# Attention, then a gated MLP, on one core: smaller transposed pieces at the start, a transposing DMA replaced by matmuls, the last product in two halves

## The chip, the cores and the metric
The kernel runs on one core of a Trainium2 chip. The metric is the device time of one execution in microseconds; below it is compared as the median of several runs. Engines: TensorE (PE in the rows, its weight loads PEld), VectorE (DVE), ScalarE (ACT), GpSimd (POOL, nearly unused here) and SyncE (SP), whose queue issues nearly all DMAs.

## The reference
q, k and v are 4 batches of 12 heads, 448 positions, 64 wide, in f32. All attention weights are sigmoids, so there is no sum over a row:

```python
scores = q @ k.T / sqrt(64) - log(448)
attn = 1 / (1 + exp(-scores))
x = (attn @ v)              # to 1792 tokens x 768
xn = x / sqrt(mean(x*x) + 1e-6) * rms_g
g = xn @ w_gate             # 768 x 1536
out = (silu(g) * (xn @ w_val)) @ w_out   # 1536 x 768
```

## The kernel before
Matmul operands are split into a high and a low f16 part, and a product of two such pairs takes three matmuls (`PARTS`: high by high, high by low, low by high).

**Attention** (0 to 139 us). The 48 heads are 12 units of four heads; a unit has 7 slots (c), and a slot's scores are 12 matmuls on 64-row quarters of the array into two PSUM banks, read by one sigmoid of 896 columns on ScalarE (L278). Slots are taken in pairs over all 84: scores of two slots, then attention times v (`av`, L289) for the two slots of the pair before. With 7 slots to a unit, (4,6) and (5,0) are one pair. After each slot's scores the list `FILL[c]` runs what is due in that slot, most of it for a unit two ahead: splitting q and k of that unit into high and low (`qk_hi`, `qk_lo`, L223 and L227, VectorE), issuing the DMA that transposes them (`transpose`, L232, SP), and issuing loads. For unit 0, `transpose_here` transposes raw f32 q and k by matmuls with an identity (L244), evicts the high part on ScalarE (L248) and makes the low part on VectorE (L249). For the units in `ON_PE` (q and k of 1, q of 2) `on_pe` transposes the split halves by f16 matmuls, 4 blocks and then 3 (`PIECES`), and copies the high part on ScalarE (L260) and the low part on VectorE (L258); each call takes 0.5 from `credit[0]`. Small PSUM results (transposes, `av` sums, norms) share four banks (tag "m"); a unit's `av` holds two of them.

After each slot and each `av`, `run_later` adds 0.8 to `credit[0]` (at most 2.5) and 0.18 to the credit of ScalarE's parts (at most 0.6), and takes parts from three queues (sums of squares, norms, weight splits) as long as the credit is above zero. The norm of one batch: sums of squares on TensorE (`squares`, L342), small steps on VectorE, a matmul that spreads the reciprocal root (`rows`, L380, copied by ScalarE at L381), then scaling and splitting (L384 on). Weight splits put the high part on ScalarE (L485).

**The MLP** (to the end). Products by a Winograd scheme for w_gate and w_val (L511) from 142 us, then 8 plain output products (L600), then five pairs of token tiles with w_out by the same scheme (`product_o`, L697). `pair_rest` runs a pair's products into banks "ob", "od" and "oc"; VectorE adds each to `u` (L736), and `store` issues the halves of the tile as two DMAs. The last product of the last pair, `product(pc, 6, 2, True)`, adds to bank "oc", which product (3, 3) began; its store goes out by SP and by ScalarE's queue.

Of the kernel before, what the change touches and what calls it, by code (L numbers as in the profile page):

```python
# [12 lines left out]
AF = mybir.ActivationFunctionType  # L13
ALU = mybir.AluOpType


SQ = 2.0**6
# [7 lines left out]
def attention_then_swiglu(  # L25
# [21 lines left out]
    nc = tc.nc  # L47
    B, H, S, D = q.shape
    DFF, DM = w_out.shape
    P = 128  # L50
    NPAIR = H // 2
    NSLOT = 2 * S // P
# [5 lines left out]
    HALF = DM // 2  # L58
# [8 lines left out]
    ps_m = ctx.enter_context(tc.tile_pool(name="ps_m", bufs=4, space=bass.MemoryType.PSUM))  # L67

    WARM, BETWEEN = 6, 2
    SPLIT_AT = (12, 30)  # L70
    ON_PE = ((1, 0), (1, 1), (2, 0))
    PIECES = (0, 4), (4, 3)
    MID = 3
    SLOT = 0.8
    ACT_SLOT = 0.18

# [6 lines left out]
    ident = const.tile([P, P], F32, name="ident")  # L83
# [90 lines left out]
    def bank(name):  # L174
        return ps_m.tile([P, 512], F32, tag="m", name=name)
# [4 lines left out]
    stt = nc.vector.scalar_tensor_tensor  # L180
# [3 lines left out]
    at, pav = {}, {}  # L184
# [44 lines left out]
    def transpose(u, t):  # L229
        if (u, t) in ON_PE:  # L230
            return
        nc.sync.dma_start_transpose(  # L232
            out=t_b[u % 3][:, t].rearrange("p l c r -> p (l c) r"),
            in_=nat(u)[:, t].rearrange("p l c d -> p (l c d)"),
        )

    def transpose_here(u, t):
        src, dst = raw(u, t), t_b[u % 3][:, t]
        ps = [bank("tr") for _ in range(2)]
        for c in range(NSLOT):  # L240
            half_, at = divmod(c, MID + 1)
            for r in range(2):
                o = ps[half_][D * r : D * r + D, at * P : at * P + P]
                nc.tensor.matmul(o, src[:, r, c], ident, start=True, stop=True)  # L244
        for half_ in range(2):
            n = MID + 1 - half_
            hi, lo = (dst[:, l, half_ * (MID + 1) : half_ * (MID + 1) + n].rearrange("p c r -> p (c r)") for l in range(2))
            nc.scalar.activation(hi, ps[half_][:, : n * P], AF.Copy, scale=SQ)  # L248
            stt(lo, ps[half_][:, : n * P], SQ, hi, ALU.mult, ALU.subtract)  # L249

    def on_pe(u, t, begin, n):
        for l in range(2):
# [253 lines left out]
    def product(ps, fc, n, a, b, more=False):  # L506

        w = win[fc % 2]
        for c in range(NK):
            for m, (l, r) in enumerate(PARTS):  # L510
                nc.tensor.matmul(  # L511
                    ps,
                    w[:, l, b, c],
                    xc[n, a][:, r, c],
                    start=(not more and c == 0 and m == 0),
                    stop=(c == NK - 1 and m == 2),
                    skip_group_check=more,
                )
# [136 lines left out]
    def sums_h(p, t):  # L655

        f11, f12, f21, f22 = hf_b
        s22, s11, s21, s12 = hs_b[p % 2]

        def add(o, f0, f1, op, cost):  # L660
            return lambda: tt(o, f0, f1, op), cost

        def hi(s, f):
            return lambda: nc.scalar.activation(s[:, 0], f, AF.Copy), 0.0

        parts = []
        for f, tile_, i in ((f21, t + 1, 0), (f22, t + 1, 1), (f11, t, 0), (f12, t, 1)):
            for m, k, parts_ in h_whole(tile_, i):
                parts.append(add(f[:, m : m + k], *parts_, ALU.add, 0.1 + 0.14 * k))
        parts += [add(f22, f21, f22, ALU.add, 0.97), hi(s22, f22)]  # L670
        parts += [add(f21, f11, f21, ALU.subtract, 0.97), hi(s21, f21)]
        parts += [add(f11, f22, f11, ALU.subtract, 0.97), hi(s11, f11)]
        parts += [add(f12, f12, f11, ALU.subtract, 0.97), hi(s12, f12)]
        los = [add(s[:, 1], f, s[:, 0], ALU.subtract, 0.91) for s, f in ((s11, f11), (s21, f21), (s22, f22), (s12, f12))]
        return [(x, cost, ("f", p)) for x, cost in parts] + [(x, cost, (p, n)) for n, (x, cost) in enumerate(los)]
# [10 lines left out]

    unit_o = 1.0 / (SH * SO)

    def product_o(p, t, ps, x, y, more=False):
        def a(m, l):  # L690
            return hs_b[p % 2][x - 3][:, l, m] if x > 2 else h_part(2 * m + (x > 0), l, t + (x == 2))

        w, i, e = (
            (wo, 0, 0), (wo, 1, 0), (wo, 1, 1), (wt, 0, 0), (wt, 0, 1), (wt, 1, 1), (wt, 1, 0))[y]
        for m in range(NFC // 2):
            for n, (l, r) in enumerate(PARTS):
                nc.tensor.matmul(  # L697
                    ps[:, :HALF],
                    a(m, l),
                    w[2 * m + i][:, r, e * HALF : e * HALF + HALF],  # L700
                    start=(not more and m == 0 and n == 0),
                    stop=(m == NFC // 2 - 1 and n == 2),
                    skip_group_check=more,
                )
# [20 lines left out]
    def pair_rest(p, t):  # L725

        def product(ps, x, y, more=False):
            if x in (4, 5, 3, 6):
                run_line((p, (4, 5, 3, 6).index(x)))
            product_o(p, t, ps, x, y, more)  # L730
            clock["pe"] += HALF_PROD
            run_line()
            clock["dve"] = max(clock["dve"], clock["pe"]) + 0.56

        def add(o, ps, u):
            stt(two(o), two(ps[:, :HALF]), unit_o, u, ALU.mult, ALU.add)  # L736

        u = u_o[p]
        c22, c21, c12 = (next_o() for _ in range(3))
        pb = bank("ob")  # L740
        product(pb, 4, 5)
        stt(u, two(pb[:, :HALF]), unit_o, u, ALU.mult, ALU.add)
        pd, pc = banks("od")[:, 0], banks("oc")[:, 0]
        product(pd, 5, 4)
        add(c22, pd, u)
        product(pc, 3, 3)
        add(c22, pc, two(c22))
        store(c22, t + 1, 1)
        product(pd, 2, 6, True)
        add(c21, pd, u)  # L750
        store(c21, t + 1, 0)
        product(pc, 6, 2, True)
        add(c12, pc, u)
        store(c12, t, 1, True)

    n_out = [0]

# [6 lines left out]
        nc.scalar.activation(o, ps[:, :HALF], AF.Copy, scale=unit_o)  # L764
        store(o, t, e)

    def store(o, t, e, last=False):
        cols = slice(e * HALF, e * HALF + HALF)
        rows = out.rearrange("(b p c) d -> b c p d", b=B, c=NSLOT)
        for j in range(2):  # L770
            b, c = divmod(2 * t + j, NSLOT)
            queue = nc.scalar if last and j else nc.sync
            queue.dma_start(rows[b ^ 1, c, :, cols], o[64 * j : 64 * j + 64])


    adds, norms, splits = [], [], []
# [24 lines left out]
    def ahead_by(n, part, *t, cost=0.0):  # L801
        def run(u):
            if u + n < NU:
                part(u + n, *t)
                credit[0] -= cost

        return run

    K, Q = 1, 0
# [5 lines left out]
    def only(n, part, *which, cost=0.0):  # L815
        def run(u):
            if u == n:
                part(*which)
                credit[0] -= cost

        return run

    def from_1(n, part, *t, cost=0.0):
        run = ahead_by(n, part, *t, cost=cost)
        return lambda u: u and run(u)

    def first(*parts):
        return [only(0, x, *a, cost=cost) for x, *a, cost in parts]

    def second(*parts):  # L830
        return [only(1, x, *a, cost=cost) for x, *a, cost in parts]
# [4 lines left out]
        [from_1(2, qk_hi, Q, cost=0.53)],  # L836
        first((on_pe, 1, Q, *PIECES[0], 0.0)) + [next_v, from_1(2, qk_lo, Q, cost=1.0)],
        first((on_pe, 1, Q, *PIECES[1], 0.0), (qk_hi, 2, K, 0.53)) + [from_1(2, transpose, K)],
        first((on_pe, 1, K, *PIECES[0], 0.0), (qk_lo, 2, K, 1.0)) + second((on_pe, 2, Q, *PIECES[0], 0.0)),
        first((transpose, 2, K, 0.0)) + second((on_pe, 2, Q, *PIECES[1], 0.0)) + [from_1(2, transpose, Q), ahead_by(4, load_qk, K), from_1(4, load_qk, Q)],  # L840
    )

    make_identity(nc, ident)
# [6 lines left out]
    with tc.manual_schedule():  # L850
# [19 lines left out]
        for t in (K, Q):  # L870
            for _ in range(3):
                run_load()
            load_qk(3, t)

        transpose_here(0, Q)
        warm(BETWEEN)
        transpose_here(0, K)

        todo = [(u, c) for u in range(NU) for c in range(NSLOT)]
        split = {}  # L880
        for n in range(0, len(todo) + 2, 2):
# [12 lines left out]
            if loads and loads[0][0] < 2:  # L894
                run_load()
            if n in SPLIT_AT:
                fc = SPLIT_AT.index(n)
                split[fc] = split_w(fc)
# [60 lines left out]
        first = [(t, e) for t in range(4) for e in range(2)]  # L959
# [8 lines left out]
        for c in range(NFC):  # L968
# [10 lines left out]
                    load_o(c + 10)  # L979
            else:  # L980
                run_lo()
        pairs_o = (4, 6, 8, 10, 12)
        clock.update(pe=-1.2, dve=-11.0)
        waiting = []
        for m in range(NFC // 2):
# [2 lines left out]
                sums.extend(pair)  # L988
            line.extend((x, cost, "o") for x, cost in sums)
            waiting = los  # L990
        h0 = sums_h(0, pairs_o[0])
        line.extend(h0[:2] + [(x, cost, "o") for x, cost in waiting] + h0[2:])
        for p, t in list(enumerate(pairs_o))[1:]:
            line.extend(sums_h(p, t))
        run_line()
        for (t, e), ps in zip(first, pss):
# [1 line left out]
        clock["pe"] = 0.0  # L998

        raw = None  # L1000
        for p, t in enumerate(pairs_o):
            ps = raw_first(p, t)
            if raw:
                raw_second(*raw)
            raw = p, t, ps
        raw_second(*raw)
        for p, t in enumerate(pairs_o):
            pair_rest(p, t)


# [28 lines left out]
```

## Time and profile before

| | us |
|---|---|
| median of 3 runs | 582.74 (581.82 to 583.57) |
| the profiled execution | 582.68 |
| its span, first to last record | 580.90 |
| TensorE busy | 569.7 (98%) |
| VectorE busy | 487.0 (84%) |
| ScalarE busy | 257.7 (44%) |

The span is what the rows count from (0 is its start); 1.78 us of the profiled execution lie around it. Busy shares are averages over stages with different limits: ScalarE is near full in parts of attention and nearly idle later. "L278" is line 278 of the kernel. A name such as `sc<-xc` says what an instruction writes and reads; an arrow behind the idle time names what ended it.

### The profile page before, as it was taken

What the parts mean: (1) busy time and instruction counts of PE and PEld (TensorE: products, weight loads), DVE (VectorE), ACT (ScalarE), POOL (GpSimd) and SP (SyncE); (2) the same over time, 40 slices, a digit from 0 to 9 for tenths busy, and PEclk for the clock granted to TensorE, in tenths of its full rate; (3) what the DMA queues carried; (4) which work ended last, traced back from release to release, by engine and by line L of the source; (5) the groups of instructions that cost most, each with busy time, mean ns of one, the idle gap of its engine ahead of it and who ended that gap; (6) DMA issues with size and microseconds to landing.
All of it is one profiled execution on the core that took longest, in us unless ns stands there. A gap on an engine that the chain in (4) does not pass through costs nothing.

```text
span 580.9 us, 10382 instructions
## 1 busy us (share of the span) xinstructions
PE 569.7 (98%) x4266; PEld 311.2 (54%) x4266; DVE 487.0 (84%) x746; ACT 257.7 (44%) x376; POOL 0.7 (0%) x6
## 2 busy tenths in 40 slices
PE   8999989999999999999999999999999999999996
PEld 5455545554555555555555555555556666665664
DVE  4597898988999978888788887887789999888861
ACT  5788899976643243232332423314222354411220
POOL 0000000000000000000000000000000000000000
PEclk9999999999999999999999999999999999999999
DMA  7999999980003304134041230422173023111111
GB/s 250 229 266 233 230 288 228 161 195 1 1 1 107 93 20 109 29 80 109 1 110 48 61 109 2 108 68 88 64 299 136 1 48 88 42 42 41 42 42 41
DMA packets 70881, 59.72 MB, mean 103 GB/s; under 512 B 38063, under 2 KB 69298, under 8 KB 70834
## 3 DMA queue, kind: packets, MB, share of 16 engines
q1 hardware_dynamic: 70434, 58.58, 40.7%
q8 instruction: 33, 0.54, 0.4%
q10 hardware_dynamic: 400, 0.49, 0.2%
q14 instruction: 14, 0.11, 0.1%
HBM read 44.83 MB, written 5.51 MB: 87 GB/s over the span
## 4 chain that ended last, share of the span: by engine, by line
PE 89%; ACT 5%; DVE 2%; DMA 2%; issue 2%; SPq 0%; ACTq 0%; DVEq 0%
PE cc L511 14%; PE cd L511 14%; PE ca L511 14%; PE o L600 8%; PE av L289 7%; PE cb L511 7%; PE sc L274 5%; PE oc L697 5%; PE od L697 5%; PE oa L697 5%; ACT room L278 3%; PE ob L697 3%; DMA room<-in_k_dram 1%; DMA xc<-in_k_dram 1%; ACT room L309 1%
## 5 line engine op out<-in xcount | busy, mean ns | idle before, releaser
L511 PEld LDWEIGHTS <-wr 128*128 128x128 f16 x1512 | 147.8, 98 | 138.4 <-issue 0.7
L511 PE MATMUL ca<-xc,wr 128*128 128x448 f16 x432 | 89.6, 352 | 0.0
L278 ACT ACTIVATE room<-sc,bias_s 128x896 f32<-128x896 f32 x84 | 83.3, 1031 | 13.6 <-PE sc L274 13.2
L289 PE MATMUL av<-room 64*64 64x448 f32 x672 | 74.4, 538 | 0.0
L511 PE MATMUL cc<-xc,wr 128*128 128x448 f16 x324 | 67.2, 352 | 0.0
L511 PE MATMUL cd<-xc,wr 128*128 128x448 f16 x324 | 67.2, 352 | 0.0
L274 PE MATMUL sc<-xc 64*64 64x448 f16 x1008 | 60.8, 351 | 3.8 <-ACT room L278 2.0
L274 PEld LDWEIGHTS <-xc 64*64 64x64 f16 x1008 | 33.3, 106 | 34.3 <-issue 24.3
L539 ACT ACTIVATE room<-ca 128x448 f32<-128x448 f32 x24 | 13.0, 542 | 84.8 <-PE ca L511 84.8
L511 PE MATMUL cb<-xc,wr 128*128 128x448 f16 x216 | 44.8, 352 | 0.0
L488 DVE SCALAR_TENSOR_TENSOR wr<-wr 128x768 f16<-128x768 f32 (+1 forms) x48 | 39.1, 852 | 2.2 <-ACT wr L485 2.2
L289 PEld LDWEIGHTS av<-room 64*64 64x64 f32 x672 | 28.1, 133 | 21.6 <-issue 16.0
L600 PE MATMUL o<-xc,room 128*128 128x384 f16 x240 | 39.2, 326 | 0.0
L566 ACT ACTIVATE room<-room 128x448 f32<-128x448 f32 x24 | 13.8, 576 | 52.9 <-DVE room L565 52.9
L485 ACT ACTIVATE wr<-wr 128x768 f16<-128x768 f32 (+1 forms) x48 | 34.8, 763 | 4.9 <-DVE wr L482 4.9
L697 PEld LDWEIGHTS <-wr 128*128 128x128 f16 x246 | 24.1, 98 | 15.9
L600 PEld LDWEIGHTS <-room 128*128 128x128 f16 x240 | 23.5, 98 | 15.6
L534 DVE TENSOR_TENSOR room<-room,cb 128x448 f32<-128x448 f32 x24 | 14.9, 620 | 16.8 <-PE cb L511 16.7
L435 DVE SCALAR_TENSOR_TENSOR wr<-wr 128x768 uint32<-128x768 uint32 x28 | 26.8, 957 | 0.8
L434 DVE SCALAR_TENSOR_TENSOR wr<-wr 128x768 uint32<-128x768 uint32 x28 | 26.8, 958 | 0.6
L697 PEld LDWEIGHTS <-room 128*128 128x128 f16 x204 | 20.0, 98 | 13.2
L527 ACT ACTIVATE room<-ca 128x448 f32<-128x448 f32 x24 | 13.1, 544 | 30.2 <-PE ca L511 24.6
(161 smaller groups left out, 751.9 us busy)
## 6 DMA issues: line engine op xcount, KB each, us to landing
room<-in_v_dram SPq DMA_DIRECT2D x24, 224.0 KB, 4.5
wr<-in_moe_w_gate_dram SPq DMA_DIRECT2D x12, 384.0 KB, 3.7
wr<-in_moe_w_gate_dram SPq DMA_DIRECT2D x24, 192.0 KB, 4.2
wr<-in_moe_w_val_dram SPq DMA_DIRECT2D x12, 384.0 KB, 4.3
wr<-in_moe_w_val_dram SPq DMA_DIRECT2D x24, 192.0 KB, 4.5
wr<-in_moe_w_out_dram SPq DMA_DIRECT2D x6, 768.0 KB, 5.0
xc<-in_k_dram SPq DMA_DIRECT2D x20, 224.0 KB, 3.7
xc<-in_q_dram SPq DMA_DIRECT2D x20, 224.0 KB, 4.3
```

Source lines behind the costliest of these rows:

```text
L274: nc.tensor.matmul(o, T[rows, 1, l, c, cols], T[rows, 0, m, :, cols], start=(n == 0), stop=(n == 2))
L278: nc.scalar.activation(a, ps[:, :, :S], AF.Sigmoid, bias=bias_s, scale=1.0 / (math.sqrt(D) * SQ * SQ))
L289: nc.tensor.matmul(ps[D * (j ^ r) : D * (j ^ r) + D, :S], v_b[u % 2][rows, r, c], a[rows, r], start=(c == 0), stop=(c == NSLOT - 1),)
L434: lambda: stt(b, r[:, :, 0], 29, b, ALU.logical_shift_right, ALU.bitwise_or),
L435: lambda: stt(b, r[:, :, 1], 0xC0000000, b, ALU.bitwise_and, ALU.bitwise_or),
L485: nc.scalar.activation(t[:, 0, s], wf[:, s], AF.Copy, scale=SW)
L488: stt(t[:, 1, s], wf[:, s], SW, t[:, 0, s], ALU.mult, ALU.subtract)
L511: nc.tensor.matmul(ps, w[:, l, b, c], xc[n, a][:, r, c], start=(not more and c == 0 and m == 0), stop=(c == NK - 1 and m == 2), skip_group ...
L534: tt(u_b, u_b, pb[:, :S], ALU.add)
L566: nc.scalar.activation(y[:, 1], y[:, 1], AF.Silu, scale=UNIT)
L600: nc.tensor.matmul(ps[:, :HALF], h[c, t // NTOK][:, l, t % NTOK * P : t % NTOK * P + P], wo[c][:, r, e * HALF : e * HALF + HALF], start=(c ...
L697: nc.tensor.matmul(ps[:, :HALF], a(m, l), w[2 * m + i][:, r, e * HALF : e * HALF + HALF], start=(not more and m == 0 and n == 0), stop=(m ...
```

## The change
Three edits. (1) `transpose_here` takes a piece (a first block and a count) and one bank for each; q of unit 0 is taken in its pieces of 4 and 3 blocks, k in 2, 3 and 2. (2) (5, 0), q of unit 5, joins `ON_PE`: its DMA transpose is not issued, and `on_pe` runs for it in unit 4, in slots 5 and 6. (3) The last product of the last pair is made as two products of 192 columns, each followed by its add and its store.

```diff
-    ON_PE = ((1, 0), (1, 1), (2, 0))
+    ON_PE = ((1, 0), (1, 1), (2, 0), (5, 0))
...
-    def transpose_here(u, t):
+    def transpose_here(u, t, begin, n):
         src, dst = raw(u, t), t_b[u % 3][:, t]
-        ps = [bank("tr") for _ in range(2)]
-        for c in range(NSLOT):
-            half_, at = divmod(c, MID + 1)
+        ps = bank("tr")
+        for c in range(n):
             for r in range(2):
-                o = ps[half_][D * r : D * r + D, at * P : at * P + P]
-                nc.tensor.matmul(o, src[:, r, c], ident, start=True, stop=True)
-        for half_ in range(2):
-            n = MID + 1 - half_
-            hi, lo = (dst[:, l, half_ * (MID + 1) : half_ * (MID + 1) + n].rearrange("p c r -> p (c r)") for l in range(2))
-            nc.scalar.activation(hi, ps[half_][:, : n * P], AF.Copy, scale=SQ)
-            stt(lo, ps[half_][:, : n * P], SQ, hi, ALU.mult, ALU.subtract)
+                o = ps[D * r : D * r + D, c * P : c * P + P]
+                nc.tensor.matmul(o, src[:, r, begin + c], ident, start=True, stop=True)
+        hi, lo = (dst[:, l, begin : begin + n].rearrange("p c r -> p (c r)") for l in range(2))
+        nc.scalar.activation(hi, ps[:, : n * P], AF.Copy, scale=SQ)
+        stt(lo, ps[:, : n * P], SQ, hi, ALU.mult, ALU.subtract)
...
-        product(pc, 6, 2, True)
-        add(c12, pc, u)
-        store(c12, t, 1, True)
+        if p + 1 < len(PAIRS_O):
+            product(pc, 6, 2, True)
+            add(c12, pc, u)
+            store(c12, t, 1, True)
+        else:
+            for n in range(2):
+                cols = slice(n * HALF // 2, (n + 1) * HALF // 2)
+                product_o(p, t, pc, 6, 2, True, cols)
+                stt(c12[:, cols], pc[:, cols], unit_o, u[:, n], ALU.mult, ALU.add)
+                store(c12, t, 1, True, cols)
...
-        first(...) + second((on_pe, 2, Q, *PIECES[0], 0.0)),
+        first(...) + second((on_pe, 2, Q, *PIECES[0], 0.0)) + [only(4, on_pe, 5, Q, *PIECES[0])],
-        first(...) + second((on_pe, 2, Q, *PIECES[1], 0.0)) + [from_1(2, transpose, Q), ...],
+        first(...) + second((on_pe, 2, Q, *PIECES[1], 0.0)) + [only(4, on_pe, 5, Q, *PIECES[1]), from_1(2, transpose, Q), ...],
...
-        transpose_here(0, Q)
+        for piece in PIECES:
+            transpose_here(0, Q, *piece)
         warm(BETWEEN)
-        transpose_here(0, K)
+        for piece in ((0, 2), (2, 3), (5, 2)):
+            transpose_here(0, K, *piece)
```

`product_o` and `store` take the columns as an argument, and the list of pairs of the last stage moves to the top as `PAIRS_O`.

## Rows read from the trace of the kernel before

**Rows 1.** The page: busy time and share by engine; chain of waits, shares by engine.
```profile
PE 569.7 (98%) x4266; PEld 311.2 (54%) x4266; DVE 487.0 (84%) x746; ACT 257.7 (44%) x376; POOL 0.7 (0%) x6
...
PE 89%; ACT 5%; DVE 2%; DMA 2%; issue 2%; SPq 0%; ACTq 0%; DVEq 0%
```

**Rows 2.** Chain of waits, 0 to 145 us: start us, us, engine and line.
```profile
7.28 1.10 PE tr L244 x15
...
9.78 0.41 PE sc L274 x4
...
10.21 1.91 ACT room L278 x2
```

**Rows 3.** Waits, 44 to 48 us: who for whom, total us, times, longest.
```profile
PEld av L289 <- DMA room<-in_v_dram: 1.2, 2, 0.7
```

**Rows 4.** Line 232, 46.5 to 47.5 us: the transpose of unit 4's q.
```profile
DMA to landing us min/median/max: 5.7/5.7/5.7
```

**Rows 5.** Timeline of TensorE, 40 to 92 us: start, us, instructions, idle before and releaser.
```profile
52.64 1.42 PE L274 MATMUL sc<-xc 64*64 64x448 f16 x24
...
63.09 0.76 PE L274 MATMUL sc<-xc 64*64 64x448 f16 x12
64.89 0.76 PE L274 MATMUL sc<-xc 64*64 64x448 f16 x12 [1.04 <-DMA xc<-room]
...
82.17 0.76 PE L274 MATMUL sc<-xc 64*64 64x448 f16 x12 [0.48 <-ACT room L278]
...
85.22 1.66 PE L274 MATMUL sc<-xc 64*64 64x448 f16 x24 [0.78 <-ACT room L278]
```

**Rows 6.** Timeline of SP, 40 to 130 us: issues only, not the transfers.
```profile
58.25 2.54 SPq L232 DMA_TRANSPOSE xc<-room  x1
61.25 1.27 SPq L191 DMA_DIRECT2D xc<-in_k_dram  x2
```

**Rows 7.** Timelines of VectorE and of TensorE, 92 to 145 us.
```profile
130.02 3.03 DVE L384 TENSOR_TENSOR room<-room 128x1344 f32<-128x1344 f32 x2 [1.34 <-ACT room L381]
...
141.63 0.95 PE L342 MATMUL ssq<-ones,room 128*112 128x1 f32 x8 [0.70 <-DVE room L312]
```

**Rows 8.** Lines 255, 248, 249, 697, whole span: ns min/median/max, first and last start, forms.
```profile
L255 PE MATMUL tr<-room x42: 216/219/230, 12.9 to 30.8; 128*128 128x128 f16 x42
...
L248 ACT ACTIVATE xc<-tr x4: 490/544/597, 5.1 to 9.1; 128x512 f16<-128x512 f32 x2, 128x384 f16<-128x384 f32 x2
...
L249 DVE SCALAR_TENSOR_TENSOR xc<-tr,xc x4: 548/620/692, 5.7 to 9.6; 128x512 f16<-128x512 f32 x2, 128x384 f16<-128x384 f32 x2
...
L697 PE MATMUL oc<-xc,wr x63: 326/326/326, 511.5 to 576.1; 128*128 128x384 f16 x63
```

**Rows 9.** Timeline of VectorE, 50 to 92 us: the split of unit 7's k.
```profile
66.39 0.63 DVE L223 TENSOR_SCALAR room<-xc 128x896 f16<-128x896 f32 x1 [1.33 <-DMA xc<-in_k_dram]
```

**Rows 10.** Timeline of all engines, 0 to 40 us: transposes of unit 1.
```profile
12.86 0.62 PE L255 MATMUL tr<-room 128*128 128x128 f16 x8
...
15.83 1.01 ACT L278 ACTIVATE room<-sc,bias_s 128x896 f32<-128x896 f32 x1 [1.35 <-PE sc L274]
...
16.73 0.48 ACT L260 ACTIVATE xc<-tr 128x384 f16<-128x384 f32 x1
```

**Rows 11.** Timeline of ScalarE, 50 to 92 us.
```profile
63.96 1.01 ACT L278 ACTIVATE room<-sc,bias_s 128x896 f32<-128x896 f32 x1 [0.22 <-PE sc L274]
...
83.30 0.97 ACT L485 ACTIVATE wr<-wr 128x768 f16<-128x768 f32 x1
```

**Rows 12.** Timeline of all engines, 560 to 582 us: the last product and its add.
```profile
573.38 3.09 PE L697 MATMUL oc<-xc,wr 128*128 128x384 f16 x18
...
576.51 0.56 DVE L736 SCALAR_TENSOR_TENSOR room<-oc,room 128x384 f32<-128x384 f32 x1 [2.37 <-PE oc L697]
```

**Rows 13.** The page, DMA issues: count, KB each, median us to landing.
```profile
wr<-in_moe_w_out_dram SPq DMA_DIRECT2D x6, 768.0 KB, 5.0
...
out_dram<-room SPq DMA_DIRECT2D x46, 96.0 KB, 2.2
```

More of the change, by code (lines that the diff above doesn't have):

```diff
@@ L69, in attention_then_swiglu @@
     WARM, BETWEEN = 6, 2
+    PAIRS_O = (4, 6, 8, 10, 12)
     SPLIT_AT = (12, 30)
-    ON_PE = ((1, 0), (1, 1), (2, 0))
+    ON_PE = ((1, 0), (1, 1), (2, 0), (5, 0))
     PIECES = (0, 4), (4, 3)
-    MID = 3
     SLOT = 0.8
@@ L687, in attention_then_swiglu, with product_o @@
     unit_o = 1.0 / (SH * SO)
-    def product_o(p, t, ps, x, y, more=False):
+    def product_o(p, t, ps, x, y, more=False, cols=slice(0, HALF)):
         def a(m, l):
@@ L697, in product_o @@
                 nc.tensor.matmul(
-                    ps[:, :HALF],
+                    ps[:, cols],
                     a(m, l),
-                    w[2 * m + i][:, r, e * HALF : e * HALF + HALF],
+                    w[2 * m + i][:, r, e * HALF + cols.start : e * HALF + cols.stop],
                     start=(not more and m == 0 and n == 0),
@@ L765, in out_end, with store @@
         store(o, t, e)
-    def store(o, t, e, last=False):
-        cols = slice(e * HALF, e * HALF + HALF)
+    def store(o, t, e, last=False, part=slice(0, HALF)):
+        cols = slice(e * HALF + part.start, e * HALF + part.stop)
         rows = out.rearrange("(b p c) d -> b c p d", b=B, c=NSLOT)
@@ L772, in store @@
             queue = nc.scalar if last and j else nc.sync
-            queue.dma_start(rows[b ^ 1, c, :, cols], o[64 * j : 64 * j + 64])
+            queue.dma_start(rows[b ^ 1, c, :, cols], o[64 * j : 64 * j + 64, part])
     adds, norms, splits = [], [], []
@@ L838, in attention_then_swiglu @@
         first((on_pe, 1, Q, *PIECES[1], 0.0), (qk_hi, 2, K, 0.53)) + [from_1(2, transpose, K)],
-        first((on_pe, 1, K, *PIECES[0], 0.0), (qk_lo, 2, K, 1.0)) + second((on_pe, 2, Q, *PIECES[0], 0.0)),
-        first((transpose, 2, K, 0.0)) + second((on_pe, 2, Q, *PIECES[1], 0.0)) + [from_1(2, transpose, Q), ahead_by(4, load_qk, K), from_1(4, load_qk, Q)],
+        first((on_pe, 1, K, *PIECES[0], 0.0), (qk_lo, 2, K, 1.0)) + second((on_pe, 2, Q, *PIECES[0], 0.0)) + [only(4, on_pe, 5, Q, *PIECES[0])],
+        first((transpose, 2, K, 0.0)) + second((on_pe, 2, Q, *PIECES[1], 0.0)) + [only(4, on_pe, 5, Q, *PIECES[1]), from_1(2, transpose, Q), ahead_by(4, load_qk, K), from_1(4, load_qk, Q)],
     )
@@ L981, in attention_then_swiglu @@
                 run_lo()
-        pairs_o = (4, 6, 8, 10, 12)
         clock.update(pe=-1.2, dve=-11.0)
@@ L990, in attention_then_swiglu @@
             waiting = los
-        h0 = sums_h(0, pairs_o[0])
+        h0 = sums_h(0, PAIRS_O[0])
         line.extend(h0[:2] + [(x, cost, "o") for x, cost in waiting] + h0[2:])
-        for p, t in list(enumerate(pairs_o))[1:]:
+        for p, t in list(enumerate(PAIRS_O))[1:]:
             line.extend(sums_h(p, t))
@@ L1000, in attention_then_swiglu @@
         raw = None
-        for p, t in enumerate(pairs_o):
+        for p, t in enumerate(PAIRS_O):
             ps = raw_first(p, t)
@@ L1006, in attention_then_swiglu @@
         raw_second(*raw)
-        for p, t in enumerate(pairs_o):
+        for p, t in enumerate(PAIRS_O):
             pair_rest(p, t)
```

## The prediction, made before the changed kernel was run
> **What bounds the kernel now.** I read the page's busy shares and the chain of waits first: TensorE is busy 98% of the span and carries 89% of the chain [rows 1]. From about 142 us to the end the chain is nothing but matmuls, each product following the one before. Nothing in the change touches that stretch but its last product. So the question is what happens in three places: the start (unit 0), the attention stage around units 4 and 5, and the last 10 us. The order of work on each engine is written by hand, so the small steps matter: what TensorE waits for, and which engine's queue holds that up.
>
> In the start the chain goes through the load of unit 0's k, its transposes, one eviction on ScalarE and one VectorE pass, and then the first sigmoids [rows 2]. Between there and 60 us the transfers are the slow part. At 45 to 46 us weight loads of unit 3 wait 1.2 us in all for v [rows 3], and q of unit 4, transposed by a DMA issued at 46.76, lands 5.7 us later [rows 4], at 52.46, with unit 4's first scores starting at 52.64 [rows 5]. Then comes the one plain idle gap that the change is about: scores of (4,6) start at 63.09 and are through at 63.85, those of (5,0) start at 64.89, and the 1.04 us between is put down to the transposing DMA [rows 5]. That DMA is q of unit 5, issued at 58.25 [rows 6]. Two later gaps, 0.48 and 0.78 us, are ended by sigmoids on ScalarE [rows 5]. At the end of attention TensorE waits 0.70 us for VectorE's sums of squares [rows 7].
>
> **Part 1, unit 0.** q keeps its pieces of 4 and 3 blocks, so nothing moves there. k goes from 4+3 to 2+3+2 blocks. The transposes stay (an f32 matmul is two records; 15 records take 1.10 us [rows 2]); one more eviction and one more VectorE pass are added, none of them long. An eviction of 512 columns costs ScalarE 0.60 and of 384 columns 0.49, the VectorE pass 0.69 and 0.55 [rows 8]; by the same step per 128 columns, 256 columns cost 0.38 and 0.41. The first piece is 8 records, two of which ran before 7.28, so it is done at about 7.85, evicted by 8.25, and its low part ready at 8.7. TensorE is through the transposes at about 8.8. So the first scores no longer break off until 9.78 [rows 2]: 12 matmuls, 0.76 us with their latency (the scores of (4,6) show it [rows 5]), and the first sigmoid starts at 9.6 in place of 10.21. That is 0.6 us earlier, and until 44 us I see nothing that stops it. But then v of unit 3 and q of unit 4 come by DMA. The transfers are not moved, and the margin at unit 4's first scores is 52.64 − 52.46 = 0.18 us. I take 0.1 us as the part that gets through; the ends are 0 and 0.6.
>
> **Part 2, q of unit 5.** Removed: one DMA transpose, 2.54 us of SP's time at 58.25 [rows 6]; the loads behind it (k of unit 7 at 61.25 first) go out about 3 us earlier, and VectorE's wait of 1.33 us for that k [rows 9] goes. That gain is off TensorE's path; it makes room for VectorE's two copies below (0.69 and 0.55 us by the like pass [rows 8]). Added: in unit 4, slot 5, eight f16 matmuls of 128 columns, and in slot 6 six more, with a copy to f16 on ScalarE and one on VectorE for each group.
>
> The same operation stands in the trace for units 1 and 2. Eight such matmuls take 0.62 us from first start to last end [rows 10], one of them 0.219 [rows 8]; with the change between 64-row and whole-array matmuls I count 0.6 us, as TensorE is busy on both sides. So the scores of (4,6) start at 63.7, not 63.09, and their sigmoid at 64.56, not 63.96 [rows 11].
>
> What matters is the second group. Slot (4,6) is the first of its pair and (5,0) the second, so the six matmuls and their evictions stand straight before the scores that need them, with no attention-times-v work between. On ScalarE the copy of the high part is queued behind the sigmoid of (4,6). In unit 0 the same order shows its price: sigmoid at 15.83, copy at 16.73 for 0.48 [rows 10], so the copy ends 1.38 us after the sigmoid began; with 0.04 for the release (576.47 to 576.51 in [rows 12]) that is 1.42. Here it gives 64.56 + 1.42 = 65.98 for the first matmul of (5,0), against 64.89 now: **+1.1 us**. VectorE's copy of the low part has to wait for nothing longer. So the DMA wait goes, and a wait of about its size for ScalarE comes in its place, on top of the matmuls added. Ends: −0.05 if the copy is never late (1.04 saved, about 1.0 of matmuls added), and +1.4 if VectorE's copy comes last.
>
> The rest follows from the queue of deferred work. Each group takes 0.5 from the credit by which the norms and weight splits are dealt out (0.8 a call, at most 2.5). Stepping that rule through the code, the reciprocal root of the first norm stays where it is, behind (4,3), but ScalarE's parts of the second weight split move from behind (6,1) and (6,3) to behind the scores of (6,6) and (7,0). One such part costs ScalarE 0.97 us at 83.30 [rows 11], just ahead of the wait of 0.78 us at 85.22 [rows 5]. That wait should go, and a smaller one, some 0.3 us, come in unit 7, where two such parts now fall in one pair: −0.5, ends −0.8 and 0.
>
> Against that, the third norm's step that spreads the reciprocals moves from behind (10,5) to behind the scores of (11,1), a call (0.6 us) later. VectorE waits for it now (1.34 us before 130.02) and then works without a break until TensorE, already idle for 0.70, gets the squares at 141.63 [rows 7]. A later start there is a longer wait here: +0.45, ends 0 and +0.6.
>
> **Part 3, the last product.** 18 matmuls of 384 columns become twice 18 of 192. Now: first start 573.38, last end 576.47, VectorE's add 0.56 from 576.51 [rows 12]; the store then goes out. Streaming: one 384-column matmul lasts 0.326 [rows 8], so the others follow at (3.09 − 0.326)/17 = 0.163, or 0.054 for 128 columns of the same rate; the 128-column ones run at (0.62 − 0.219)/7 = 0.057 [rows 8, 10], so weight loads add only 0.003. 192 columns: 0.081 + 0.003 = 0.084 each, 0.27 for a single one (halfway between 0.219 and 0.326), 1.70 us for a half. The add of 192 columns: 0.56 less 1.5 times 0.14 [rows 8], 0.35.
>
> Does the second half wait for the first half's add? Both halves lie in one PSUM bank, and the trace has no matmul that writes one part of a bank while another engine reads another. Bounds: no wait, or the add plus its release, 0.35 + 0.1. In the rows there are matmuls that hold until a bank's reader is done (the scores of 82.17 and 85.22 for the sigmoid [rows 5]), and that is the nearest; I take the wait. The first half then ends at 575.08, its add at 575.47, the second half runs 575.52 to 577.22, its add to 577.61: 0.54 later than now (577.07). Without the wait the second half ends at 573.38 + 35 × 0.084 + 0.27 = 576.59 and its add at 576.98, 0.1 earlier. The last store is half as large: 768 KB land in 5.0 us and 96 KB in 2.2 [rows 13], 0.2 for 48 KB. The saving lies between 0 and 0.4 (two such stores share the way out); I take 0.2. Part 3: **+0.3**, ends −0.5 and +0.5.
>
> The Trainium skill speaks to this (PSUM — Partial Sum Buffer, "PSUM bank collisions raise a hardware error"): TensorE writing and VectorE reading one bank in the same quadrant at once is an error even at different columns, so accesses must be guarded by bank. By that rule the halves can't overlap, and the sum is the one below; without it, it would be 0.63 less, 583.3. No row of this trace shows which holds.
>
> **Sum.** −0.1 + 1.1 − 0.5 + 0.45 + 0.3 = +1.25 us. The profiled execution took 582.68 us (span 580.90 and 1.78 around it), 0.06 from the median of the runs, so the forecast is 582.68 + 1.25 = 583.9. What a measurement here can tell from no change is about 0.3%, 1.75 us: so no change that can be told.
>
> **Rivals.**
> A. *The new wait is hidden.* If ScalarE takes the copy ahead of time, or TensorE's shift at (5,0) is swallowed later because the sigmoids set the pace to 89 us, part 2 is about 0. For: ScalarE is the releaser of both later gaps. Against: its queue is in order and starts that stretch when TensorE lets it. 582.68 − 0.1 + 0 + 0.3: 582.9. Chance 0.25.
> B. *Slower: VectorE at the end of attention.* If the third norm's spreading slips by two more calls, behind (11,0), VectorE starts 1.3 us later still, and as it has no break before 141.63, TensorE idles 2.5 us there and not 0.7: 583.9 + 1.3 = 585.2. It decides from a slip of two calls on (585.0 and more). For: no slack between 130 and 141 us. Against: my stepping gives one call. Chance 0.17.
> C. *The halves overlap and the early start gets through.* The last add ends 0.1 earlier and the head's 0.6 is kept: 583.9 − 0.6 − 0.5 = 582.8. Against: rows 3 and 4 for the head. Chance 0.13; a little of it (all gains at their best, below 581.0) is faster.
>
> The forecast has 0.45. All lows together give 580.7, all highs 585.2; the range **581.4 to 585.3** leaves out about 2 in 10. Faster by over 0.3%: 0.06; within: 0.75; slower: 0.19 (B and the forecast's upper edge).
>
> **What would show it.** Right: the first sigmoid near 9.6; the scores of (5,0) waiting for ScalarE's copy (not a DMA) and starting near 66; no ScalarE gap of 0.78 near unit 6's end; a wait above 1 us for VectorE before the squares at about 142; in the last product, a gap of about 0.45 us between two runs of 18 matmuls, ended by VectorE. Wrong: (5,0) starting before 65, no gap in the last product, or the matmul stage beginning before 139.

## The result and the profile after

Seven runs of each kernel on one chip: 585.54 us median after (583.79 to 587.05) against 581.93 before (580.72 to 583.57), a ratio of 1.0061 [1.0044, 1.0078]. That is slower by 3.6 us, outside the range that was given, and by more than the 0.3% that the forecast called no change.

The profiled execution of the changed kernel took 584.69 us with a span of 582.6; the one before took 582.68 with 580.9. The shares look alike: the page's busy times and, from its chain of waits, the shares by engine.

```profile
PE 571.6 (98%) x4298; PEld 313.7 (54%) x4298; DVE 488.1 (84%) x750; ACT 259.0 (44%) x379; POOL 0.7 (0%) x6
...
PE 84%; DVE 7%; ACT 5%; issue 2%; DMA 1%; SPq 0%; ACTq 0%; DVEq 0%
```

TensorE still has 98%, as in [rows 1]. In the chain VectorE has 7% where it had 2%, and TensorE 84% where it had 89%; ScalarE's 5% is unchanged. The difference is in a few short places. (Lines of the changed kernel are up to three lower than before in the attention code: the spread's copy, L381 before, is L378 here.) The timeline of the changed kernel's TensorE, with a few lines of ScalarE and VectorE (start in us, duration, instructions, and in brackets the idle time before them and who ended it):

```profile
9.69 3.77 ACT L275 ACTIVATE room<-sc,bias_s 128x896 f32<-128x896 f32 x4 [0.31 <-PE sc L271]
...
52.27 1.33 PE L271 MATMUL sc<-xc 64*64 64x448 f16 x24
...
60.78 0.62 PE L252 MATMUL tr<-room 128*128 128x128 f16 x8
...
63.48 0.76 PE L271 MATMUL sc<-xc 64*64 64x448 f16 x12
64.17 0.51 PE L252 MATMUL tr<-room 128*128 128x128 f16 x6
...
64.35 1.01 ACT L275 ACTIVATE room<-sc,bias_s 128x896 f32<-128x896 f32 x1 [0.22 <-PE sc L271]
65.26 0.48 ACT L257 ACTIVATE xc<-tr 128x384 f16<-128x384 f32 x1
...
65.79 0.76 PE L271 MATMUL sc<-xc 64*64 64x448 f16 x12 [1.11 <-ACT xc L257]
...
83.08 0.76 PE L271 MATMUL sc<-xc 64*64 64x448 f16 x12 [0.39 <-ACT room L275]
...
85.40 1.66 PE L271 MATMUL sc<-xc 64*64 64x448 f16 x24
```

The six matmuls of unit 5's second piece are through at 64.68. The copy to f16 that the next scores need starts on ScalarE at 65.26, because the sigmoid of (4,6) holds that engine from 64.35, and TensorE waits 1.11 us for it. In [rows 5] a DMA ended a wait of 1.04 us at this place. Of the two later gaps there, the one of 0.78 us is gone, and the one of 0.48 has become 0.39.

Then the end of attention, from the same view:

```profile
130.00 0.55 PE L377 MATMUL rinv<-room,ones 112*128 112x448 f16 x2
130.18 1.01 ACT L275 ACTIVATE room<-sc,bias_s 128x896 f32<-128x896 f32 x1 [0.73 <-PE sc L271]
131.09 0.54 ACT L378 ACTIVATE room<-rinv 128x448 f32<-128x448 f32 x1
131.66 3.03 DVE L381 TENSOR_TENSOR room<-room 128x1344 f32<-128x1344 f32 x2 [2.59 <-ACT room L378]
139.52 1.88 PE L508 MATMUL ca<-xc,wr 128*128 128x448 f16 x9
143.15 0.95 PE L339 MATMUL ssq<-ones,room 128*112 128x1 f32 x8 [1.75 <-DVE room L309]
143.95 1.86 PE L508 MATMUL cb<-xc,wr 128*128 128x448 f16 x9
```

The spread of the third norm's reciprocals (L377) stands one call later, as forecast. But its copy (L378) now comes behind a sigmoid that started 0.18 us after the two matmuls, so VectorE gets it late: it waits 2.59 us, against 1.34 in [rows 7], has no break afterwards, and TensorE waits 1.75 us for the sums of squares where it waited 0.70. The same places in the kernel before, where ScalarE was free when the spread came:

```profile
128.85 0.55 PE L380 MATMUL rinv<-room,ones 112*128 112x448 f16 x2
129.44 0.54 ACT L381 ACTIVATE room<-rinv 128x448 f32<-128x448 f32 x1 [0.58 <-PE rinv L380]
139.05 1.88 PE L511 MATMUL ca<-xc,wr 128*128 128x448 f16 x9
```

Last, the end of the kernel: timeline of TensorE and VectorE, and the DMA issues (KB each, median us from issue to landing):

```profile
574.90 1.65 PE L694 MATMUL oc<-xc,wr 128*128 128x192 f16 x18
576.59 0.36 DVE L757 SCALAR_TENSOR_TENSOR room<-oc,room 128x192 f32<-128x192 f32 x1 [0.93 <-PE oc L694]
577.00 1.65 PE L694 MATMUL oc<-xc,wr 128*128 128x192 f16 x18 [0.45 <-DVE room L757]
578.68 0.36 DVE L757 SCALAR_TENSOR_TENSOR room<-oc,room 128x192 f32<-128x192 f32 x1 [1.74 <-PE oc L694]
...
out_dram<-room ACTq DMA_DIRECT2D x2, 48.0 KB, 2.1
```

The halves run one after the other with 0.45 us between them. From the first matmul to the end of the last add it is 4.14 us; before it was 3.69 (573.38 to the end of the add in [rows 12]).

Laid end to end, profiled execution against profiled execution:

| Stretch | forecast | measured |
|---|---|---|
| start to unit 4's first scores (52.64 to 52.27) | −0.1 | −0.37 |
| from there to the scores of (5,0) (64.89 to 65.79) | +1.1 | +1.27 |
| from there to the first product of the next stage (139.05 to 139.52) | −0.5 | −0.43 |
| from there to the squares (141.63 to 143.15) | +0.45 | +1.05 |
| from there to the last product (573.38 to 574.90) | 0 | 0.00 |
| last product, add and store to the span's end | +0.3 | +0.18 |
| around the span (1.78 to 2.09) | 0 | +0.31 |
| sum | +1.25 | +2.01 |

That leaves 1.6 us of the 3.6 between the medians. 0.75 of it is the kernel before: its profiled execution lay that far above the median of these seven runs. The other 0.85 is the kernel after: its median lies that far above its profiled execution. Its seven times fall into two groups by the mean granted clock of TensorE: 583.79, 584.32, 584.69 and 585.54 us at 1.000, and 586.84, 587.00 and 587.05 at 0.997. Together with the six runs of the first experiment, five of 13 executions are at 0.997 with a median of 586.8, and eight at 1.000 with one of 584.7: 2.1 us apart. The kernel before, in 73 executions on the chips of the experiments, has one below 0.998.

### The profile page after: what moved, and what is told of

Read it like the earlier page. It is cut to its first block, busy times and chain, and to the rows that moved or that the text cites. A ratio compares the mean times of both kernels' runs of the same rounds, so it can differ in the third digit from the quotient of the medians.

```text
span 582.6 us, 10457 instructions
## 1 busy us (share of the span) xinstructions
PE 571.6 (98%) x4298; PEld 313.7 (54%) x4298; DVE 488.1 (84%) x750; ACT 259.0 (44%) x379; POOL 0.7 (0%) x6
## 4 chain that ended last, share of the span: by engine, by line
PE 84%; DVE 7%; ACT 5%; issue 2%; DMA 1%; SPq 0%; ACTq 0%; DVEq 0%
PE cc L508 14%; PE cd L508 14%; PE ca L508 14%; PE o L597 8%; PE cb L508 7%; PE oc L694 5%; PE od L694 5%; PE oa L694 5%; PE av L286 4%; ACT room L275 3%; PE sc L271 3%; PE ob L694 3%; DVE room L227 1%; DVE room L381 1%; DVE room L309 1%
```

## The experiments

Theory A: most of the unforeseen time comes from the 0.5 that each new group of transposes takes from the credit. It moves the third norm's spread behind a sigmoid; the longer wait before the squares costs a microsecond directly, and in a share of the executions TensorE's clock drops after it. Theory B, the rival: it comes from unit 5's new transposes themselves and from the halved product, whatever the credit does. The ratios below lie close to those of the mean times, so a few long executions move them more than they move the medians; where the two part, both are given.

**The changed kernel once more.** No edit; a second profile and more runs.

> The changed kernel once more, nothing edited, to see how its executions spread. Of its 7 executions 3 took 586.84 to 587.05 us with a mean granted clock of 0.997 and 4 took 583.79 to 585.54 with 1.000. Theory A (the longer wait before the squares at the end of attention, 1.75 us against 0.70, in some executions brings TensorE's clock down for a stretch): again a third to a half of the executions near 587 at 0.997, the rest near 584.5; if the profile falls on one, the clock is below 1.00 in a stretch that begins at about 143 us. Theory B (the clock falls by chance, wherever it is): no such grouping, the kernel before shows it as often, or the stretch lies elsewhere.

585.26 us (584.67 to 586.49, 6 runs), 1.0051 [1.0035, 1.0068]. Two of the six at a clock of 0.997, and those are the slowest two (586.49, 586.18). The wait before the squares is 1.75 us again, at (5,0) 1.11 again. The profiled execution was one of those at full clock, so the drop itself was not caught.

**Part 2 alone on the kernel before.**

```
-    ON_PE = ((1, 0), (1, 1), (2, 0))
+    ON_PE = ((1, 0), (1, 1), (2, 0), (5, 0))
...
-second((on_pe, 2, Q, *PIECES[0], 0.0)),
+second((on_pe, 2, Q, *PIECES[0], 0.0)) + [only(4, on_pe, 5, Q, *PIECES[0])],
...
-second((on_pe, 2, Q, *PIECES[1], 0.0)) + [from_1(2, transpose, Q),
+second((on_pe, 2, Q, *PIECES[1], 0.0)) + [only(4, on_pe, 5, Q, *PIECES[1]), from_1(2, transpose, Q),
```

> The kernel before with only q of unit 5 on TensorE. Theory A (this part carries the whole loss): scores of (5,0) wait for ScalarE's copy about 1.1 us and start near 66.2 (before 64.89, no head gain), the squares at about 143.3 after a wait of about 1.75, span 580.9 + 1.9 = 582.8, and again executions at a clock of 0.997; ratio to before 1.005 to 1.007. Theory B (the last product's halves carry it): ratio within 1.002.

585.64 us (7 runs), 1.0057 [1.0035, 1.008] without the longest: part 2 alone brings the whole loss. That longest one is the profiled execution, with late transfers at the start (592.88 us), so its time says nothing, but it shows the clock falling twice: to 0.50 from 63.5 to 66.9 after TensorE had idled 2.52 us for v, and from 152.2 to 155.6 after 1.75 us idle before the squares.

**The change without part 2.**

```
-    ON_PE = ((1, 0), (1, 1), (2, 0), (5, 0))
+    ON_PE = ((1, 0), (1, 1), (2, 0))
```
(and both calls of `only(4, on_pe, 5, Q, ...)` taken out)

> The changed kernel without its second part: unit 0's k in three pieces and the last product in halves, q of unit 5 by DMA again. Theory A: first sigmoid near 9.7 (before 10.21), the lead gone at (5,0) since that DMA lands when it did (within 0.3 us of 64.89), squares' wait back to 0.70, last add 0.45 later than before and the store 0.25 shorter: span 580.9 to 581.2, ratio 0.999 to 1.001, all executions at a clock of 1.000. Theory B (the halves' gap near the end brings the clock down or costs more than seen): ratio 1.003 or more.

581.67 us (580.48 to 585.92, 12 runs), 0.9997 [0.998, 1.0014], one of the 12 at a clock of 0.997. The waits are back to the old ones (TensorE's timeline):

```profile
65.03 0.76 PE L271 MATMUL sc<-xc 64*64 64x448 f16 x12 [0.23 <-DMA xc<-room]
...
141.80 0.95 PE L339 MATMUL ssq<-ones,room 128*112 128x1 f32 x8 [0.69 <-DVE room L309]
```

The wait for the DMA itself is 0.23 us in this execution and 1.04 in [rows 5]: what part 2 can save there is not the same each time.

**The credit kept: all of the change, but unit 5's groups take nothing from it.**

```
-        credit[0] -= 0.5
+        credit[0] -= 0.5 * (u < 5)
```

> The changed kernel, but the two groups of matmuls for unit 5 take nothing from the credit, so that the deferred work is dealt out behind the same slots as in the kernel before. Theory A: (5,0) still waits 1.1 us for ScalarE's copy and starts near 65.8; ScalarE's gap of 0.78 near 85 us comes back, so attention ends 0.3 to 0.4 us later than in the changed kernel; but the squares wait only about 0.7 again: span 580.9 + 0.9 + 0.2 = 582.0 (changed: 582.6), no execution at 0.997, ratio about 1.002. Theory B: the wait before the squares has nothing to do with the clock: ratio as for the changed kernel, 1.005 to 1.007, a third or more of the executions at 0.997.

584.17 us (584.03 to 588.62, 10 runs), 1.0057 [1.0034, 1.0079]. The squares wait 0.69 again, and six of ten spans are 581.9 to 582.1, as A said: by the medians it is 2.0 us above the kernel before, against 3.1 for the changed kernel on the same chip. But the ratio, for which A expected 1.002, is no lower than the changed kernel's 1.0051: four of the ten executions are 2 to 4.6 us above the others. Two of them are at a clock of 0.997 (spans 586.5 and 586.1), which A had not expected; two more, at 0.999, have spans of 584.2 and 585.7. The first of these two is the profiled one, and its TensorE waits for v:

```profile
59.46 2.06 PE L286 MATMUL av<-room 64*64 64x448 f32 x14 [1.70 <-DMA room<-in_v_dram]
...
144.75 0.95 PE L339 MATMUL ssq<-ones,room 128*112 128x1 f32 x8 [0.69 <-DVE room L309]
```

There a late transfer costs the time, and the granted clock stays at 1.00 up to the last product. So the credit explains the wait before the squares, not every drop of the clock and not every long execution.

**The debit alone on the kernel before.** No transpose is moved; two calls in unit 4 take 0.5 each from the credit.

```
+    def debit():
+        credit[0] -= 0.5
...
-second((on_pe, 2, Q, *PIECES[0], 0.0)),
+second((on_pe, 2, Q, *PIECES[0], 0.0)) + [only(4, debit)],
...
-second((on_pe, 2, Q, *PIECES[1], 0.0)) + [from_1(2, transpose, Q),
+second((on_pe, 2, Q, *PIECES[1], 0.0)) + [only(4, debit), from_1(2, transpose, Q),
```

> The kernel before, with 0.5 taken from the credit in slots 5 and 6 of unit 4 and nothing else: no matmuls, no copies, q of unit 5 by DMA. Theory A (the debit moves the third norm's spread one call back and, on ScalarE, behind one sigmoid more): scores of (5,0) as before, 64.9; attention's last products 0.3 to 0.5 us earlier than before (ScalarE's relief), but the squares at the end wait about 1.75 us in place of 0.70 and start near 142.3; span 581.5, and in some executions (about a third) a clock of 0.997, 2 us longer; ratio 1.002 to 1.004. Theory B (the longer wait comes from the late (5,0), that is from the matmuls): squares wait 0.7, ratio 0.999 to 1.001.

584.28 us (581.78 to 588.6, 12 runs), 1.0031 [1.0012, 1.005]. Arithmetic on a list makes the kernel slower, with no work added. The profile has the long wait:

```profile
63.40 0.76 PE L274 MATMUL sc<-xc 64*64 64x448 f16 x12 [0.20 <-DMA xc<-room]
...
140.76 0.95 PE L342 MATMUL ssq<-ones,room 128*112 128x1 f32 x8 [1.75 <-DVE room L312]
```

Eight of its 12 executions have a clock of 0.997 or less, with a median of 584.9 us; the three at 1.000 have one of 582.1. The profiled one is of the three. From its scores of (5,0) to the squares it is 77.36 us, where the kernel before has 76.74 (64.89 to 141.63): at full clock the debit costs 0.62 us there, the longer wait less what the gap of 0.78 us near unit 6's end gives back. (That its span, 580.0, is even below that of the kernel before is the transfers' doing: the wait for the DMA at (5,0) is 0.20 us here and 1.04 there.) Most of the 1.8 us between the medians goes with the clock. Theory B has no place for this.

**The idle time filled.** The debit alone, and ahead of the last norm's squares 24 matmuls of constants into the bank of the squares; what they write is overwritten.

```
+            for _ in range(24 * (b == 3)):
+                nc.tensor.matmul(ps[0][:, :P], ones16, ones16, start=True, stop=True)
             for t in range(4):
```

> The debit alone, as before, with 24 extra f16 matmuls of 128 columns on constants (1.3 us, their result is overwritten) ahead of the last norm's squares, so that TensorE works through most of its wait for VectorE. Theory A (TensorE's idling there brings its clock down): squares start where they did with the debit alone (about 140.8 to 142.3), idle before them under 0.5 us, no execution at 0.997 or below where 9 of 12 were, times 581.8 to 583, ratio 0.999 to 1.001. Theory B (the clock falls for another reason): as many executions at 0.997, ratio 1.003.

(The count quoted there for the debit alone is one too high: it is eight of 12, a ninth is at 0.998.) 582.56 us (581.67 to 583.73, 12 runs), 1.0003 [0.9988, 1.0018], every clock 0.998 or more. TensorE's timeline:

```profile
138.20 1.88 PE L513 MATMUL ca<-xc,wr 128*128 128x448 f16 x9
139.91 1.50 PE L342 MATMUL ssq<-ones 128*128 128x128 f16 x24
141.82 0.95 PE L344 MATMUL ssq<-ones,room 128*112 128x1 f32 x8 [0.41 <-DVE room L312]
```

The squares come no earlier; TensorE only has something to do until 0.41 us before them. The drops go with the idle time, and with them the loss: the drop follows from the idle, not from the debit. One reservation: these executions ran on another chip than the debit alone, which was not repeated there. That this chip too drops its clock after the long wait is shown by the next run, made on it.

**The last product whole again**, the rest of the change kept; a single execution.

```
-        if p + 1 < len(PAIRS_O):
-            product(pc, 6, 2, True)
...
+        product(pc, 6, 2, True)
+        add(c12, pc, u)
+        store(c12, t, 1, True)
```

> The changed kernel with the last product whole. Theory A: as the changed kernel up to the last product (squares' wait 1.75), last add 3.7 us after the last product's start, and the time around the span as in the changed kernel, 2.1 us, if it comes from the matmuls of unit 5 with the pieces of k. Theory B (the 0.3 us around the span comes from the last product's halves): 1.8 us around the span.

585.57 us, clock 0.996. From the last product's start to the last add's end it is 3.68 us, as before the change, and the time around the span is 1.8 us, as theory B had it; but the change without part 2 has the halves, and 1.8 too, so the halves alone don't make it 2.1. And this profile caught a drop. TensorE's timeline, and then busy time by stretch (stretch, its length, busy time and instructions of PE, PEld, DVE, ACT and POOL, the granted clock, DMA share, GB/s):

```profile
143.01 0.95 PE L339 MATMUL ssq<-ones,room 128*112 128x1 f32 x8 [1.75 <-DVE room L309]
143.82 2.32 PE L508 MATMUL cb<-xc,wr 128*128 128x448 f16 x9
145.94 3.13 PE L508 MATMUL cd<-xc,wr 128*128 128x448 f16 x9
149.29 1.87 PE L508 MATMUL cc<-xc,wr 128*128 128x448 f16 x9
```
```profile
144.00:145.00 1.00, 1.00 (x7) 0.53 (x6) 0.83 (x6) 0.00 (x0) 0.00 (x0) 1.00 0.00 0
145.00:146.00 1.00, 1.00 (x5) 0.41 (x4) 0.83 (x6) 0.00 (x0) 0.00 (x0) 0.54 0.00 0
146.00:147.00 1.00, 1.00 (x4) 0.38 (x3) 1.00 (x3) 0.00 (x0) 0.00 (x0) 0.50 0.00 0
147.00:148.00 1.00, 1.00 (x4) 0.44 (x3) 0.74 (x2) 0.00 (x0) 0.00 (x0) 0.50 0.07 16
148.00:149.00 1.00, 1.00 (x6) 0.44 (x4) 0.00 (x0) 0.00 (x0) 0.00 (x0) 0.75 0.00 0
149.00:150.00 1.00, 1.00 (x7) 0.49 (x6) 0.62 (x1) 0.52 (x1) 0.00 (x0) 1.00 0.00 0
```

After 1.75 us idle, two runs of nine matmuls take 2.32 and 3.13 us in place of 1.87: 0.45 and 1.26 us more, 1.7 of the 2.1 that part the two groups of executions. The granted clock says why: 0.50, the level of 1.2 GHz. TensorE counts as fully busy in these rows; busy share alone doesn't show it.

**The copy first.** The credit kept, and the second group of transposes issued ahead of the scores of (4,6), so that its copy no longer stands behind their sigmoid.

```
+                if (u, c) == (4, 6):
+                    on_pe(5, Q, *PIECES[1])
                 scores(u, c)
```
(and the call of `on_pe` for that group taken out of the list of slot 6)

> The changed kernel with the credit kept, and the second group of unit 5's matmuls ahead of the scores of (4,6) and not behind them, so that ScalarE's copy stands ahead of the sigmoid of (4,6). Theory A (the wait at (5,0) is the copy queued behind that sigmoid): no wait of 1.11 us at (5,0); a smaller one, up to 0.4 us, before the group's low half for a bank; (5,0) starts about 0.6 us earlier than with the credit kept alone, undisturbed span 581.4 (credit kept: 582.0), ratio 1.000 to 1.002. Theory B (the matmuls themselves and the bank of the spread set it): (5,0) no earlier, span 582.0.

583.23 us (582.49 to 588.4, 12 runs), 1.003 [1.001, 1.0051]. TensorE's timeline:

```profile
62.68 0.55 PE L377 MATMUL rinv<-room,ones 112*128 112x448 f16 x2
63.07 0.33 PE L252 MATMUL tr<-room 128*128 128x128 f16 x3
63.86 0.33 PE L252 MATMUL tr<-room 128*128 128x128 f16 x3 [0.46 <-ACT room L378]
64.12 1.33 PE L271 MATMUL sc<-xc 64*64 64x448 f16 x24
```

The scores of (4,6) and (5,0) are one run of 24. The wait of 1.11 us is gone; one of 0.46, ended by the spread's copy (L378), stands in its place. The time above the kernel before falls from 2.0 us (credit kept) to 0.8 by the medians, and from 3.4 to 1.7 by the means. Even so the kernel is no faster than before: the transposes on TensorE are still paid. Two of 12 are at 0.997 here too.

**The last product's halves in two banks of one tile**, on the change without part 2; the two products that share that sum are both halved.

```
-        pd, pc = banks("od")[:, 0], banks("oc")[:, 0]
+        pd, pcs = banks("od")[:, 0], banks("oc")
...
+                product_o(p, t, pcs[:, n], 6, 2, True, cols)
+                stt(c12[:, cols], pcs[:, n, cols], unit_o, u[:, n], ALU.mult, ALU.add)
```

> Parts 1 and 3 of the change, with the last product's halves in two PSUM banks (product (3,3) of the last pair, which they add to, is halved as well). Theory A (the gap of 0.45 us between the halves is the one bank): no gap, the second half straight behind the first, last add ends about 0.1 us earlier after the start of the last product than in the kernel before (3.6 us) and not 0.45 later (4.14); span 0.45 below that of parts 1 and 3, ratio 0.998 to 1.000. Theory B (the second half waits for its weights or the store): the gap stays.

582.82 us (580.91 to 584.05, 12 runs), 1.0005 [0.9991, 1.0019]. The expectation failed, the gap stays as it was:

```profile
571.39 1.65 PE L694 MATMUL oc<-xc,wr 128*128 128x192 f16 x18
573.07 0.36 DVE L764 SCALAR_TENSOR_TENSOR room<-oc,room 128x192 f32<-128x192 f32 x1 [0.93 <-PE oc L694]
573.48 1.65 PE L694 MATMUL oc<-xc,wr 128*128 128x192 f16 x18 [0.45 <-DVE room L764]
```

**The halves in two tiles**, each with its own bank.

```
-        pd, pcs = banks("od")[:, 0], banks("oc")
-        pc = pcs[:, 0]
+        pd, pc = banks("od")[:, 0], banks("oc")[:, 0]
+        pcs = pc, bank("oc2") if p + 1 == len(PAIRS_O) else None
```

> As the two banks, but the second half of the last product (and of the product that it adds to) writes a PSUM tile of its own, where before both banks were of one tile. Theory A (the wait between the halves is kept for a tile, and a bank of its own in a tile of its own ends it): no gap between the halves, last add ends 3.6 us after the last product's start (4.14 with one bank or one tile), span 0.5 below the two banks', ratio 0.998 to 1.000. Theory B (something else holds the second half): the gap of 0.45 stays.

581.32 us (580.09 to 583.65, 12 runs), 0.9975 [0.9955, 0.9996]: the one version below the kernel before by more than its interval, if only by a quarter of a per cent. (It ran on another chip than the two banks; what decides is the gap in the trace, not the times.)

```profile
572.33 3.13 PE L694 MATMUL oc<-xc,wr 128*128 128x192 f16 x36
574.01 0.36 DVE L764 SCALAR_TENSOR_TENSOR room<-oc,room 128x192 f32<-128x192 f32 x1 [0.93 <-PE oc L694]
575.50 0.36 DVE L764 SCALAR_TENSOR_TENSOR room<-oc,room 128x192 f32<-128x192 f32 x1 [1.13 <-PE oc L694]
```

36 matmuls without a break; the last add ends 3.53 us after the first of them began, against 4.14 in the change and 3.69 before it.

## Why the prediction was wrong

**The head (−0.1).** Right in place, too small in size. The first sigmoid starts at 9.69 (forecast 9.6, before 10.21), and 0.37 us of it gets through to unit 4, inside the ends of 0 and 0.6 but not the 0.1 chosen. Where part 2 is left out the first sigmoid is at 10.02, so of 0.5 us part comes and goes between executions. What the pieces themselves give can be read where k's 28 transposes run unbroken in 1.75 us: from their start to the first sigmoid it is 2.95 us with two pieces (the idle time filled, 7.55 to 10.50) and 2.50 with three (the changed kernel, 7.19 to 9.69).

**Unit 5's wait (+1.1).** Right, in mechanism and size: a wait for ScalarE's copy, 1.11 us, and 1.44 us from the sigmoid's start to (5,0) where 1.42 was forecast; from unit 4's first scores to (5,0) it is 1.27 more than before. That (5,0) starts at 65.79, even before the 65.98 forecast, is the head's 0.37. Moving the copy ahead of the sigmoid removes the wait and lowers the time. So rival A, a hidden wait, falls.

**ScalarE's relief (−0.5).** Right in size, −0.43, and in its first half: the gap of 0.78 us goes, and by the scores behind it 0.72 us is gained (from (5,0) to them it is 19.61 us, to 85.40; before it was 20.33, to 85.22). Up to 139 us 0.29 of it is lost again, but not as the wait of 0.3 us forecast for unit 7: TensorE's timeline has no such gap, and where the 0.29 goes isn't shown. The gap is the debit's doing: it goes with the debit alone, and is back (0.79) in both versions with the credit kept.

**The end of attention (+0.45, ends 0 and 0.6).** Here the sum failed first: the term was mis-sized, and its end too low; it measured +1.05. The move by one call was as stepped through; what was priced was only the 0.6 us of the call. But at the new place the spread's copy stands in ScalarE's queue behind the sigmoid of (11,1), the very order that part 2 had priced for unit 5: 1.09 us from the matmuls' start to the copy's, where the trace of before has 0.59 (128.85 to 129.44). The 0.5 us between these and the 0.6 of the call make 1.1; TensorE's wait grew by 1.05. Rival B's price (1.3 us) was nearer than the forecast's, with its condition, a slip of two calls, not met.

And the price of that wait was not the wait alone: this is the second step that failed, a cost put at nothing. Five of 13 executions of the changed kernel have a lower clock, some 2 us each, which no term and no rival had. Two profiles, of part 2 alone and of the whole last product, show the drop right behind the long wait; the debit alone and the filled idle time show that the wait brings it (in the changed kernel itself no profile caught one). In the first seven runs it lifts the median by about a microsecond: the four at full clock have one of 584.5.

**The last product (+0.3).** Right in mechanism: 0.45 us between the halves, forecast 0.45; the last add ends 0.45 later, forecast 0.54; the store gives back 0.27, forecast 0.2. But the reason given, that both halves lie in one bank, isn't what the runs bear out: with two banks in one tile the gap was the same 0.45, with two tiles it was gone. The Trainium skill's rule (PSUM — Partial Sum Buffer, "PSUM bank collisions raise a hardware error") gave the right sum here, but the gap is no evidence for it: no run here shows the two engines in one bank at once. Two tiles within one bank weren't tried.

**The sum.** 583.9 was forecast and 585.54 measured, 1.6 us more: 0.6 from the end of attention, 0.85 between the profiled execution and the median, which is put down to the clock, 0.3 around the span, and −0.15 from all other terms together. The range missed by 0.24 us, since it held rival B's price but nothing for the clock: at full clock the median would be 584.5, inside it, so the mis-sized term alone would not have carried the time out. The base was luck besides: 582.68 lay 0.75 above the median of the kernel before in the same seven runs, and from 581.93 the forecast would have been 583.2 and the miss 2.4.

Between the theories: by the medians the debit alone costs 1.8 us, where the forecast's two terms for it (−0.5 and +0.45) add up to −0.05; the change with the credit kept costs 2.0, where the other terms give 1.3, and 0.3 of the rest lies around the span. So most of what was not foreseen is the debit's, as A has it, but not all.

What stays open: the 0.3 us around the span. It is 2.1 us with unit 5's q on TensorE and the halved product together (after, once more, credit kept, copy first; all of them with k in three pieces), and 1.8 in all other kernels, those with one of the two among them. Nothing in the span shows why. Open too is what lowers the clock in two of ten and two of 12 executions of the two versions with the short wait before the squares; idle time from late transfers early in the kernel is a candidate, and not settled: the profile of part 2 alone shows a lower clock after 2.52 us of it, the one with the credit kept none after 1.70.

## What to carry to other kernels

Where a hand-made order deals out work by a running credit, an edit's cost is also what it pushes back: step the rule to the end of the stage, and at each new place ask what stands ahead on the queue of the engine that finishes the step, not only how many calls it moved. Price a longer idle time of TensorE above its length, read the granted clock after it in several executions, and try filling it before reordering the work. A product halved so that its add overlaps needs a tile of its own for each half.

## What the runs showed of the chip that was not expected

- An idle time of 1.75 us before the squares was followed in some executions, not in all, by a granted clock of 0.50 (1.2 GHz in place of 2.4) beginning about 2 us after TensorE had started again (squares at 143.01 and 150.29, the drop at 145.1 and 152.2), for 3.4 us. After 2.52 us idle for v the drop came 0.7 us after the restart (62.77, 63.5) and lasted as long. By the mean clock (0.997 or less), eight of 12 executions of the debit alone had a drop, none of 12, on another chip, with the idle time filled to 0.41 us. The profile of the changed kernel showed none: one profiled execution at full clock doesn't rule it out.
- The matmuls of a second half wait for the reader of the first by tile: 0.45 us in two banks of one tile, none in two tiles.
- 18 f16 matmuls of 192 columns take 1.65 us (forecast 1.70), and a store of 48 KB lands 2.1 us after its issue where one of 96 KB took 2.4.
